# VectorE's compound tasks split in the plan, one set of eight PSUM banks, and a new order for every engine

## The chip, the cores and the metric

The kernel runs on one core of a Trainium2 chip. A core has engines with an instruction stream each: TensorE (PE in the profile, its weight loads PEld), VectorE (DVE), ScalarE (ACT), GpSimd (POOL) and SyncE (SP), which issues the DMAs. [...] The metric is the device time of one execution in microseconds, the median of several runs.

## The reference

Four attention layers in the order A, B, A, B on a sequence of S = 2048 rows of D = 512, each as `x = x + layer(layernorm(x))`, with H = 32 heads of Dh = 16. A and B have weights of their own, used twice.

```python
# A: each row looks at 8 rows, 2 apart, back from itself (W, dil = 8, 2)
idx = pos[:, None] - (jnp.arange(W) * dil)[None, :]
logits = jnp.where(idx >= 0, einsum("bhsd,bhswd->bhsw", q, kg) * Dh**-0.5, -1e9)
o = einsum("bhsw,bhswd->bhsd", softmax(logits), vg)
# B: each row looks at the last 256 rows
mask = (i - j >= 0) & (i - j < 256)
p = softmax(where(mask, einsum("bhqd,bhkd->bhqk", q, k) * Dh**-0.5, -1e9))
o = einsum("bhqk,bhkd->bhqd", p, v)
# both: o reshaped to [S, D] @ wo
```

## The kernel before

The sequence is cut into chunks of C = 256 rows. For layers 0 and 1, and then for layers 2 and 3, the program runs over the 8 chunks: A of a chunk, then B of it, so there are 16 pairs of stages A0, B0 to A7, B7 and on (after a preparation of the weights in pA, pB and W). Products that need more than 16-bit precision are split into a high and a low half (names ending in h and l).

Both layers begin with `norm`: per 128 rows BN_STATS, BN_AGGR and a small TENSOR_SCALAR on VectorE (L811, L812, L813), a power on POOL (L816), one more small operation on VectorE (L819), then the normalised rows on ACT (L832), their transposes on TensorE (`pt`, L836) and the two halves (L841 on ACT, L842 on VectorE). `proj_t` and `proj_n` are the projections (`pq`, `pv`, `po`; L861 to L863 and L881 to L884).

Layer A multiplies q by eight shifted windows of k on VectorE or POOL (`pr`, L994), sums over a head's 16 elements on TensorE (`L`, L1002), takes a softmax over 8 (L1025 to L1039), spreads the weights on TensorE (`pb`, L1061), multiplies by v on VectorE (`pw`, L1074) and sums on POOL or VectorE (L1079 to L1083).

Layer B computes the scores twice. `sq` has a query on each partition and the keys along the row; it serves only to find each row's maximum. A task of it (L1169 and L1172, "scores") fills a tile of two PSUM banks, one per head. Of the three blocks of 128 keys that a block of queries can touch, one is wholly inside the window and the two outer ones are complementary triangles: COPY_PREDICATED (L1188) copies the needed half of the third into the first, and TENSOR_REDUCE (L1190) takes the maximum over the two remaining ones (`m`). In a layer's first chunk a fused operation (L1183) does both. The maxima are transposed (L1200), split (L1205 or L1207, L1210) and go by way of DRAM into extra rows of the stacked operands `stk`. `sk` (L1257 and L1259) computes the same scores with a key on each partition and the maximum already subtracted, again into two banks; ACT takes the exponential (`p`, L1263), POOL clears what is outside the window (L1272), and TensorE multiplies by v (`av`, L1289), where a column of ones yields the sum of the weights. The result leaves PSUM by ACT (`os`, L1324) and is divided on its way through DRAM (L1349, L1363), rounded into two halves (L904, L906), and goes into the output projection.

The order is not that of the code. Each piece is put into `Plan` as a task with an engine, an assumed duration in us, the values that it reads and writes, and the buffers that it touches. The table `ORDER` gives each task its place on its engine, by stage; a negative number puts it on the task's other engine (`alt`). `order()` then plays the engines through with the assumed durations and emits the tasks one by one, so that each engine's order is the table's, and the buffers are handed out in the planned order of time. `LAG` is the time until another engine sees an end, `TURN` and `TO_ROWS` what a change of the kind of matmul costs (kinds "F", "R", "C", "H": full projections, row-tiled scores, column-tiled sums, half). `IDLE` = 110 tasks of three unused matmuls (L1398) fill TensorE near the start and the end.

PSUM has eight banks. Before the change they are two pools: `q_sc`, two tiles of two banks, for `sq` and `sk`, and `q_pj`, four tiles of one bank, for everything else:

```python
for name, bufs in (("q_sc", 2), ("q_pj", 4)):
    pool(name, bufs, bass.MemoryType.PSUM)
```

A task of VectorE could hold several instructions that follow each other: L1188 and L1190 were one, of 1.06 us; so were L811 to L813; L1025 and L1026; and L1029 to L1031.

Of the kernel before, what the change touches and what calls it, by code (L numbers as in the profile page):

```python
# [424 lines left out]
LAG = {"PE": 0.23, "DVE": 0.13, "ACT": 0.16, "POOL": 0.1, "SP": 0.0}  # L425
RATE = 0.33
SLOW = 0.25
TURN, TO_ROWS = 0.09, 0.165
RECENT, WARM, EDGE = 3.4, 0.31, 0.05


# [1006 lines left out]
```

## Time and profile before

| | |
|---|---|
| median of 3 runs | 1503.04 us (1502.67 to 1504.06) |
| span of the profiled execution, first to last instruction | 1498.1 us |
| the execution's own time beside the span | not listed; the median stands 4.9 us above the span |
| mean granted TensorE clock | 0.964 of full speed |
| TensorE / VectorE / ACT / POOL busy | 1385.4 / 1248.6 / 735.9 / 672.2 us |
| HBM | 57 GB/s over the span |

An engine's row gives busy time, its share of the span and the number of instructions. A group's row gives line, engine, operation, output<-inputs, shapes and count, then busy us and mean ns of one, then idle us ahead of it and what ended that idle time. In an answer on waits, "PE sk L1257 <- DVE m L1190" means that TensorE stood idle ahead of L1257 until VectorE's L1190 had ended. "issue" is idle time for which no release is seen. In a timeline a row has start, duration, engine and operation; "x2" merges two in a row. [...]

### The profile page before, as it was taken

The numbers are of one execution on the slowest core, as the hardware profiler recorded it, in microseconds if no ns is written. First come the engines' busy times: TensorE is split into PE (matmuls) and PEld (weight loads), VectorE is DVE, ScalarE is ACT, GpSimd is POOL, SyncE is SP. The second block draws the span as 40 slices with busy tenths as digits, with TensorE's granted clock in tenths as the row PEclk, the third lists the DMA queues.
The fourth block names the chain that finished last, engine by engine and source line by source line (L and its number), as shares of the span: only waits on it lengthen the run. The fifth ranks groups of instructions, "written<-read, shape, count | busy, mean of one in ns | idle before, by whom it ended". The sixth has DMA issues, their size and how long they took to land. (4 is left out here: it accounts for less than half of the span.)

```text
span 1498.1 us, 35059 instructions
## 1 busy us (share of the span) xinstructions
PE 1385.4 (92%) x14058; PEld 779.0 (52%) x14058; DVE 1248.6 (83%) x2332; ACT 735.9 (49%) x1052; POOL 672.2 (45%) x764
## 2 busy tenths in 40 slices
PE   6899999989899999989999898989989899999988
PEld 4574636546364554636456363745536365463534
DVE  7869797988979889897988879797887979889674
ACT  5432435545455554554555434555544554554554
POOL 2505263552816435282553617274363725527232
PEclk9799979999999999999999998999989999999999
DMA  6130212222221221222122131212212221222311
GB/s 211 43 101 21 73 34 70 61 57 70 50 93 39 75 59 51 69 58 83 42 67 69 49 93 41 88 37 74 65 40 76 63 80 41 66 63 48 93 42 44
DMA packets 89218, 97.38 MB, mean 65 GB/s; under 512 B 34016, under 2 KB 60128, under 8 KB 89056
## 3 DMA queue, kind: packets, MB, share of 16 engines
q1 hardware_dynamic: 88800, 94.89, 22.4%
q8 instruction: 110, 1.80, 0.5%
q14 instruction: 52, 0.43, 0.1%
q10 hardware_dynamic: 256, 0.26, 0.1%
HBM read 50.33 MB, written 35.09 MB: 57 GB/s over the span
## 5 line engine op out<-in xcount | busy, mean ns | idle before, releaser
L1263 ACT ACTIVATE p<-sk,sclB 128x768 f32<-128x768 f32 x480 | 425.2, 899 | 321.4 <-PE sk L1259 293.2
L1272 POOL TENSOR_SCALAR_AFFINE_SELECT p<-p 128x1024 f32<-128x1024 f32 x240 | 263.7, 1104 | 550.0 <-ACT p L1263 512.2
L1190 DVE TENSOR_REDUCE m<-sq 128x2 f32<-128x512 f32 x448 | 310.3, 693 | 15.4
L1188 DVE COPY_PREDICATED sq<-maskt,sq 128x256 f32<-128x256 int16 x448 | 189.1, 422 | 94.8 <-PE sq L1172 89.2
L1289 PE MATMUL av<-p,v 128*32 128x128 f32 (+1 forms) x3840 | 198.1, 332 | 3.4 <-POOL p L1272 1.5
L994 DVE TENSOR_TENSOR pr<-kv,q 128x512 f32<-128x512 f32 x230 | 165.4, 776 | 40.1 <-ACT kv L975 31.3
L1257 PE MATMUL sk<-stk,stk 64*128 64x256 f16 x960 | 135.8, 285 | 38.9 <-DVE m L1190 23.1
L1289 PEld LDWEIGHTS av<-p,v 128*32 128x32 f32 x3840 | 105.4, 110 | 95.4 <-issue 41.4
L1074 DVE TENSOR_TENSOR pw<-pb,kv 128x1024 f32<-128x1024 f32 x128 | 152.1, 1211 | 2.2 <-PE pb L1061 1.3
L1169 PE MATMUL sq<-stk,stk 48*128 48x128 f16 (+1 forms) x896 | 113.5, 254 | 30.5 <-DVE m L1190 18.9
L1081 POOL TENSOR_TENSOR pw<-pw 128x512 f32<-128x512 f32 x101 | 128.2, 1269 | 16.9 <-DVE pw L1074 16.7
L1257 PEld LDWEIGHTS <-stk 64*128 64x128 f16 x960 | 53.2, 94 | 157.6 <-issue 96.4
L1172 PE MATMUL sq<-stk,stk 48*128 48x128 f16 (+1 forms) x1024 | 127.5, 251 | 6.7 <-DVE m L1183 5.7
L1169 PEld LDWEIGHTS <-stk 48*128 48x128 f16 x896 | 49.2, 94 | 125.8 <-issue 83.9
L1259 PE MATMUL sk<-stk,stk 64*128 64x128 f16 x960 | 108.0, 222 | 0.0
L832 ACT ACTIVATE xn<-x,rs 128x512 f32<-128x512 f32 x64 | 52.0, 813 | 76.4 <-DVE rs L819 67.2
L1082 POOL TENSOR_TENSOR pw<-pw 128x256 f32<-128x256 f32 x101 | 74.8, 740 | 7.9
L1324 ACT COPY os<-av 128x512 f32<-128x512 f32 x60 | 34.9, 582 | 83.3 <-PE av L1289 83.1
L1002 PE MATMUL L<-pr,sel 128*32 128x512 f32 x512 | 71.6, 602 | 0.3 <-DVE pr L994 0.2
L861 PE MATMUL pq<-xh,wA0h 128*128 128x256 f16 x256 | 70.8, 276 | 0.0
L861 PE MATMUL pq<-xh,wA2h 128*128 128x256 f16 x256 | 70.7, 276 | 0.1
L862 PE MATMUL pq<-xl,wA0h 128*128 128x256 f16 x256 | 70.3, 275 | 0.3 <-DVE xl L842 0.3
(187 smaller groups left out, 3123.2 us busy)
## 6 DMA issues: line engine op xcount, KB each, us to landing
stk<-re SPq DMA_DIRECT2D x256, 96.0 KB
re<-eh SPq DMA_DIRECT2D x128, 128.0 KB
re<-el SPq DMA_DIRECT2D x64, 128.0 KB
oc<-os SPq DMA_DIRECT2D x120, 64.0 KB
os<-scr SPq DMA_DIRECT2D x15, 512.0 KB
x<-in_A_x_dram SPq DMA_DIRECT2D x8, 512.0 KB
xd<-x SPq DMA_DIRECT2D x16, 256.0 KB
x<-xd SPq DMA_DIRECT2D x8, 512.0 KB
```

The source lines that it names most:

```text
L861: nc.tensor.matmul(ps[mp].t[:, i], wh, xh, start=k == 0, stop=False)
L994: E.tensor_mul(pr.t, window(kv[1].t, m, 64 * tq, 64)[:, 0], qb)
L1074: nc.vector.tensor_mul(pw.t, pb.t.unsqueeze(1).broadcast_to([P, 2, W, 64]), v)
L1081: E.tensor_add(t[:, :, 0:4], t[:, :, 0:4], t[:, :, 4:8])
L1169: nc.tensor.matmul(ps.t[:, par, 0 : (2 - qb) * P], lhs, stk[hf, bef][r, col, qb * P :], start=True, stop=True)
L1172: nc.tensor.matmul(ps.t[:, par, (2 - qb) * P : 3 * P], lhs, stk[hf, now][r, col, : (1 + qb) * P], start=True, stop=True)
L1188: nc.vector.copy_predicated(t[:, :, 0:P], maskt[:, 0:P].bitcast(I16).unsqueeze(1).broadcast_to([P, 2, P]), t[:, :, 2 * P : 3 * P])
L1190: nc.vector.tensor_reduce(out=m.t[:, :, u, qb], in_=t[:, :, 0 : 2 * P], op=ALU.max, axis=AX.X)
L1257: nc.tensor.matmul(o[:, two], k[:, jf * P : (jf + 1) * P], q, start=True, stop=True)
L1263: nc.scalar.activation(pt.t[:, :, 2 * i : 2 * i + 2].rearrange("p s m q -> p m s q"), ps.t[:, :, : 3 * P].rearrange("p m (s q) -> p m s q" ...
L1272: nc.gpsimd.affine_select(out=v, in_=v, pattern=[[0, 8], [-1 if b == 0 else 1, P]], compare_op=ALU.is_gt if b == 0 else ALU.is_ge, fill=0. ...
L1289: nc.tensor.matmul(o, v[:, jj, 17 * h : 17 * h + 32], rhs, start=z == 0 and (b == 0 or first), stop=z == 1 and b == 1, tile_position=(0, 3 ...
```

## The change

VectorE's compound tasks become one task per instruction, so that the order can put other instructions between them: L1188 (`pick`) and L1190 (`top`); BN_STATS and BN_AGGR, with L813 now one instruction for both halves instead of two; and the five instructions of layer A's softmax. The plan's own constants change with it: `AGAIN` is the extra time of a task that follows its own engine's result, and `LEAVE` replaces `TURN` and `TO_ROWS` by a cost for each kind of matmul that is left. The two PSUM pools become one tile of eight banks. A `Banks` buffer asks for one bank or two neighbouring ones, and `order()` chooses them with `find` when the task begins in the plan: the banks that come free first, and among equals a single one that has taken neighbours. All numbers of `ORDER` are new. What is computed stays the same, and `IDLE` stays 110.

```diff
 ORDER = {
-    "pA": [1, 0, 2, -4, 0, 1, 5, 4, 7, 6, 11, 5, 10, 3, -5, 4, 2, 3, 5, 9, 9, 13, 42, 10, 15, 11, 16, 6, 8, 5, -7, 10,
...
-TURN, TO_ROWS = 0.09, 0.165
+LEAVE = {"C": 0.185, "H": 0.19, "R": 0.13, "F": 0.105, "": 0.0}
+AGAIN = {"PE": 0.0, "DVE": 0.11, "ACT": 0.12, "POOL": 0.055, "SP": 0.0}
...
+class Banks(Buf):
+    def __init__(self, psum, wide, shape):
+        self.key, self.cap, self.group, self.need = "banks", 0, 0, 0
+        self.left, self.held, self.until, self.wide, self.at = 0, False, 0.0, wide, None
+        def make():
+            if wide == 2:
+                return psum[:, self.at : self.at + 2]
+            v = psum[:, self.at]
+            return v if len(shape) == 2 else v.rearrange("p (a b) -> p a b", a=shape[1])
...
+def find(banks, wide, at):
+    best, score, where = math.inf, 0, None
+    for b in range(9 - wide):
+        free = max(banks[b : b + wide])
+        if free == math.inf:
+            continue
+        t, k = max(at, free), b
+        if wide == 1:
+            side = (b > 0 and banks[b - 1] < math.inf) + (b < 7 and banks[b + 1] < math.inf)
+            k = 100 * side + 7 - b
+        if t < best - 1e-6 or t < best + 1e-6 and k < score:
+            best, score, where = t, k, b
+    return best, where
...
-                x.ready = max(x.ready, t.end if x.eng == t.eng and not t.size else landed)
+                x.ready = max(x.ready, t.end + AGAIN[t.eng] if x.eng == t.eng and not t.size else landed)
...
-                us += 0.0 if t.mode == mode else TO_ROWS if t.mode == "R" else TURN
+                us += 0.0 if t.mode == mode else LEAVE[mode]
...
-    for name, bufs in (("q_sc", 2), ("q_pj", 4)):
-        pool(name, bufs, bass.MemoryType.PSUM)
+    psum = ctx.enter_context(tc.tile_pool(name="psum", bufs=1, space=bass.MemoryType.PSUM)).tile([P, 8, 512], F32, name="banks")
...
-            plan.add("DVE", 1.0, lambda t=t: stats(t), r=[vx[t]], w=[vmv[t], vr0[t], Val(b6)])
-        plan.add("POOL", 0.72, rstd, r=vr0[:2], w=[vr0[2]])
+            plan.add("DVE", 0.61, lambda t=t: stats(t), r=[vx[t]], w=[vb6[t]])
+            plan.add("DVE", 0.11, lambda t=t: aggr(t), r=[vb6[t]], w=[vmv[t]])
+        plan.add("DVE", 0.075, spread_, r=vmv, w=[vr0[0]])
+        plan.add("POOL", 0.72, rstd, r=[vr0[0]], w=[vr0[1]])
...
-                    ps = buf("q_sc", [P, 2, 512], F32, "sc", f"sq{l}_{c}_{j}_{u}_{qb}")
+                    ps = Banks(psum, 2, [P, 2, 512])
...
+                    def pick(ps=ps):
+                        t = ps.t
+                        nc.vector.copy_predicated(t[:, :, 0:P], maskt[:, 0:P].bitcast(I16).unsqueeze(1).broadcast_to([P, 2, P]),
+                                                  t[:, :, 2 * P : 3 * P])
+
+                    if not first:
+                        vpk = Val(ps)
+                        plan.add("DVE", 0.34, pick, r=[vps], w=[vpk])
+                        vps = vpk
+                    plan.add("DVE", 0.28 + 2 * (3 * P - x0) / 960 if first else 0.61, top, r=[vps], w=[v])
```

VectorE, in stage B5 of the first pair of layers, at the maxima of its last quarter of the heads (`m_5_3`; `b_7`, `mv_7` and `xl_7` are the norm of chunk 7, `el_6` is a projection of chunk 6). Before:

```order
L811 BN_STATS b_7_8018<-x_7_7955 128x6
L812 BN_AGGR mv_7_8020<-b_7_8018 128x2
L813 TENSOR_SCALAR rs_7_8022<-mv_7_8020 128x1
L1105 SCALAR_TENSOR_TENSOR el_6_1_8064<-pq_6_1_1_7908,eh_6_1_8013 128x2x256
L1105 SCALAR_TENSOR_TENSOR el_6_1_8064<-pq_6_1_0_7916,eh_6_1_8013 128x2x256
L819 SCALAR_TENSOR_TENSOR rs_7_8022<-mv_7_8020,rs_7_8022 128x2
L1210 SCALAR_TENSOR_TENSOR mt_5_2_8051<-mr_5_2_8044,mt_5_2_8051 128x32
L1188 COPY_PREDICATED sq_5_3_3_0_8030<-maskt,sq_5_3_3_0_8030 128x2x128
L1190 TENSOR_REDUCE m_5_3_8091<-sq_5_3_3_0_8030 128x2
L1188 COPY_PREDICATED sq_5_3_0_1_8080<-maskt,sq_5_3_0_1_8080 128x2x128
L1190 TENSOR_REDUCE m_5_3_8091<-sq_5_3_0_1_8080 128x2
L842 TENSOR_TENSOR xl_7_8133<-pt_7_0_8105,xh_7_8116 128x4x128
```

The same place now; L1284 is the COPY_PREDICATED, L1280 the TENSOR_REDUCE, L888, L891 and L894 the norm's three:

```order
L891 BN_AGGR mv_7_7396<-b_7_7378 128x2
L888 BN_STATS b_7_7378<-x_7_7317 128x6
L891 BN_AGGR mv_7_7396<-b_7_7378 128x2
L894 TENSOR_SCALAR rs_7_7412<-mv_7_7396 128x2
L1198 SCALAR_TENSOR_TENSOR el_6_1_7367<-banks,eh_6_1_7353 128x2x256
L1280 TENSOR_REDUCE m_5_3_7421<-banks 128x2
L900 SCALAR_TENSOR_TENSOR rs_7_7412<-mv_7_7396,rs_7_7412 128x2
L1284 COPY_PREDICATED banks<-maskt,banks 128x2x128 x2
L1280 TENSOR_REDUCE m_5_3_7421<-banks 128x2 x2
L925 TENSOR_TENSOR xl_7_7468<-banks,xh_7_7456 128x4x128 x2
L1284 COPY_PREDICATED banks<-maskt,banks 128x2x128
L1280 TENSOR_REDUCE m_5_3_7421<-banks 128x2
```

Two copies now stand ahead of their two maxima, and a projection's remainder stands between a maximum and the copy that belongs to it; some pairs still follow each other directly.

TensorE in the same stage, where scores are put between the projections of chunk 6 (`xh_6`, weights `wB0` and `wB1`). Each row of a score stands for one of two row halves; the second of each is left out. Before:

```order
L863 MATMUL pq_6_0_0_8076<-xh_6_7877,wB0l 128x256
L1169 LDWEIGHTS stk_0_122
L1169 MATMUL sq_5_3_0_1_8080<-stk_1_123,stk_0_122 128x128
...
L1172 MATMUL sq_5_3_0_1_8080<-stk_2_124,stk_0_122 128x256
...
L861 LDWEIGHTS wB0h
L861 MATMUL pq_6_0_0_8076<-xh_6_7877,wB0h 128x256
```

Now (L1262 and L1265 are `sq`, L1356 and L1358 `sk`, L944 to L946 the projection):

```order
L946 MATMUL banks<-xh_6_7217,wB1l 128x256
L1262 LDWEIGHTS stk_0_120
L1262 MATMUL banks<-stk_1_121,stk_0_120 128x128
...
L1265 MATMUL banks<-stk_2_122,stk_0_120 128x256
...
L1356 LDWEIGHTS stk_2_119
L1356 MATMUL banks<-stk_0_117,stk_2_119 128x2x128
...
L1358 MATMUL banks<-stk_0_117,stk_2_119 128x128
...
L944 LDWEIGHTS wB1h
L944 MATMUL banks<-xh_6_7217,wB1h 128x256
```

A single score task stood between two projections; now an `sq` and an `sk` task stand together. Their tiles are two-bank parts of `banks`.

More of the change, by code (lines that the diff above doesn't have):

```diff
@@ L446, in t @@
         return self.tile
+class Banks(Buf):
[7 more added lines that the diff above has]
+            return v if len(shape) == 2 else v.rearrange("p (a b) -> p a b", a=shape[1])
+        self.make, self.tile = make, None
+def find(banks, wide, at):
[11 more added lines that the diff above has]
+    return best, where
 class Val:
@@ L504, in order @@
                 slots.setdefault(b.key, [0.0] * b.cap)
+                taken.setdefault(b.key, 0)
                 if b.need is None:
@@ L508, in order @@
         taken = dict.fromkeys(taken, 0)
+        banks = [0.0] * 8
         for q in queue.values():
@@ L520, in begins @@
                 return math.inf
-            at, need = max(until[e], t.ready), {}
+            at, need, left = max(until[e], t.ready), {}, None
             for b in t.bufs:
                 if not b.held:
+                    if b.key == "banks":
+                        left = left or banks[:]
+                        at, z = find(left, b.wide, at)
+                        if z is None:
+                            return math.inf
+                        left[z : z + b.wide] = [math.inf] * b.wide
+                        continue
                     if taken[b.key] < b.need:
@@ L538, in leave @@
                 b.until = max(b.until, landed)
-                if not b.left:
+                if not b.left and b.key == "banks":
+                    banks[b.at : b.at + b.wide] = [b.until] * b.wide
+                elif not b.left:
                     slots[b.key].append(b.until)
@@ L558, in order @@
                     b.held = True
+                    if b.key == "banks":
+                        b.at = find(banks, b.wide, now)[1]
+                        banks[b.at : b.at + b.wide] = [math.inf] * b.wide
+                        continue
                     taken[b.key] += 1
@@ L811, in stats, with aggr, spread_ @@
             nc.vector.bn_stats(b6.t[:, t], xb.t[:, t])
+        def aggr(t):
             nc.vector.bn_aggr(mv.t[:, t], b6.t[:, t])
-            nc.vector.tensor_scalar(rs.t[:, 0, t : t + 1], mv.t[:, t, 1:2], 1.0e-5, 1.0 / (XS * XS), op0=ALU.add, op1=ALU.mult)
+        def spread_():
+            nc.vector.tensor_scalar(rs.t[:, 0], mv.t[:, :, 1], 1.0e-5, 1.0 / (XS * XS), op0=ALU.add, op1=ALU.mult)
         def rstd():
@@ L821, in norm @@
         for t in range(2):
-            plan.add("DVE", 1.0, lambda t=t: stats(t), r=[vx[t]], w=[vmv[t], vr0[t], Val(b6)])
-        plan.add("POOL", 0.72, rstd, r=vr0[:2], w=[vr0[2]])
-        plan.add("DVE", 0.08, shift, r=[vr0[2], *vmv], w=[vrs])
+            plan.add("DVE", 0.61, lambda t=t: stats(t), r=[vx[t]], w=[vb6[t]])
+            plan.add("DVE", 0.11, lambda t=t: aggr(t), r=[vb6[t]], w=[vmv[t]])
+        plan.add("DVE", 0.075, spread_, r=vmv, w=[vr0[0]])
+        plan.add("POOL", 0.72, rstd, r=[vr0[0]], w=[vr0[1]])
+        plan.add("DVE", 0.08, shift, r=[vr0[1], *vmv], w=[vrs])
         for t in range(2):
-            pts = buf("q_pj", [P, 4, P], F32, "pj", f"pt{l}_{c}_{t}")
+            pts = Banks(psum, 1, [P, 4, P])
             xn = buf("pxn", [P, D], F32, "xn", f"xn{l}_{c}_{t}")
@@ L848, in proj_t @@
         d = st8[l, c]
-        ps = [buf("q_pj", [P, 2, C], F32, "pj", f"pq{l}_{c}_{s}_{mp}") for mp in range(2)]
+        ps = [Banks(psum, 1, [P, 2, C]) for mp in range(2)]
         vps = [Val(x) for x in ps]
@@ L1025, in top, with less @@
             nc.vector.tensor_reduce(out=mx.t[:, 0], in_=src_.t.rearrange("p w t -> p t w"), op=ALU.max, axis=AX.X)
+        def less():
             nc.vector.tensor_sub(e.t, src_.t, mx.t[:, 0:1].broadcast_to([P, W, 64]))
@@ L1029, in bottom, with over, scaled @@
             nc.vector.tensor_reduce(out=mx.t[:, 1], in_=e.t.rearrange("p w t -> p t w"), op=ALU.add, axis=AX.X)
+        def over():
             nc.vector.reciprocal(mx.t[:, 0], mx.t[:, 1])
+        def scaled():
             nc.vector.tensor_mul(e.t, e.t, mx.t[:, 0:1].broadcast_to([P, W, 64]))
@@ L1043, in half @@
             return v.rearrange("p (w t) -> p w t", w=W)
-        plan.add("DVE", 1.33, top, r=[vsrc], w=[vt0, vmx])
+        vrx, vov = Val(mx), Val(mx)
+        plan.add("DVE", 0.615, top, r=[vsrc], w=[vmx])
+        plan.add("DVE", 0.61, less, r=[vsrc, vmx], w=[vt0], mode="S" if c == 0 else "")
         plan.add("ACT", 0.63, lambda: nc.scalar.activation(e.t, e.t, AF.Exp, scale=scl["A", 1]), r=[vt0, vscl["A", 1]], w=[vt1])
-        plan.add("DVE", 2.33, bottom, r=[vt1, vmx], w=[ve])
+        plan.add("DVE", 0.98, bottom, r=[vt1], w=[vrx])
+        plan.add("DVE", 0.47, over, r=[vrx, vmx], w=[vov])
+        plan.add("DVE", 0.61, scaled, r=[vt1, vov], w=[ve], mode="S")
         plan.add("ACT", 0.48, lambda: nc.scalar.copy(eh.t, e.t), r=[ve], w=[veh])
@@ L1130, in layer_b @@
         for t in range(2):
-            pv = buf("q_pj", [P, D], F32, "pj", f"pv{l}_{c}_{t}")
+            pv = Banks(psum, 1, [P, D])
             vps = Val(pv)
@@ L1186, in top @@
                         else:
-                            t = ps.t
-                            nc.vector.copy_predicated(t[:, :, 0:P], maskt[:, 0:P].bitcast(I16).unsqueeze(1).broadcast_to([P, 2, P]),
-                                                      t[:, :, 2 * P : 3 * P])
-                            nc.vector.tensor_reduce(out=m.t[:, :, u, qb], in_=t[:, :, 0 : 2 * P], op=ALU.max, axis=AX.X)
-                    plan.add("DVE", 0.28 + 2 * (3 * P - x0) / 960 if first else 1.06, top, r=[vps], w=[v])
+                            nc.vector.tensor_reduce(out=m.t[:, :, u, qb], in_=ps.t[:, :, 0 : 2 * P], op=ALU.max, axis=AX.X)
+                    def pick(ps=ps):
[7 more added lines that the diff above has]
+                    plan.add("DVE", 0.28 + 2 * (3 * P - x0) / 960 if first else 0.61, top, r=[vps], w=[v])
             mr = buf("psm", [P, 32], F32, "mr", f"mr{l}_{c}_{j}")
@@ L1393 @@
     for i in range(IDLE):
-        junk = buf("q_pj", [P, 2 * P], F32, "pj", f"idle{i}")
+        junk = Banks(psum, 1, [P, 512])
         def idle(junk=junk):
             for _ in range(3):
-                nc.tensor.matmul(junk.t, selt[:, 0], selt.rearrange("p g k -> p (g k)"), start=True, stop=True)
+                nc.tensor.matmul(junk.t[:, 0 : 2 * P], selt[:, 0], selt.rearrange("p g k -> p (g k)"), start=True, stop=True)
         plan.add("PE", 0.33, idle, w=[Val(junk)], mode="F", act=0.32)
```

15 lines of the change are left out of this document (8 added, 7 removed), and 793 rows, old and new, of the table ORDER.

## The prediction

> **What bounds the kernel now.** I read the page's first part, then the stages, then TensorE's waits, then single instructions in one stretch of the middle. The page's busy line and the stages (columns as the header says; "PEld" is the weight load):
>
> ```profile
> PE 1385.4 (92%) x14058; PEld 779.0 (52%) x14058; DVE 1248.6 (83%) x2332; ACT 735.9 (49%) x1052; POOL 672.2 (45%) x764
> core 0: us, PE busy (x) PEld busy (x) DVE busy (x) ACT busy (x) POOL busy (x), PEclk, DMA share, GB/s
> 0.00:100.00 100.00, 81.31 (x553) 54.66 (x554) 75.54 (x152) 49.13 (x73) 30.28 (x58) 0.91 0.36 115
> 100.00:1400.00 1300.00, 1222.01 (x12529) 682.74 (x12527) 1112.29 (x2066) 637.65 (x916) 611.63 (x679) 0.97 0.22 61
> 1400.00:1498.10 98.10, 82.07 (x981) 41.56 (x979) 60.79 (x115) 49.09 (x63) 30.27 (x28) 0.98 0.22 61
> ```
>
> In the 1300 us of the middle TensorE is busy for 94% and VectorE for 86%; ACT and POOL are at half. No engine is full: TensorE is the bound, with 78 us in which it stands still (1300 - 1222), and VectorE is close behind. So a shorter VectorE pays only where TensorE waits for it. TensorE's waits, longest first (us in total, times, longest):
>
> ```profile
> PE sk L1257 <- DVE m L1190: 23.1, 39, 1.9
> PE sq L1169 <- DVE m L1190: 18.9, 33, 1.9
> PE sk L1257 <- ACT p L1263: 12.4, 25, 1.0
> PE sq L1169 <- ACT p L1263: 9.8, 22, 1.1
> ...
> PE sq L1172 <- DVE m L1183: 5.7, 10, 1.6
> ...
> PE sk L1257 <- DVE m L1183: 1.6, 4, 0.9
> ...
> PE sq L1172 <- ACT p L1263: 0.8, 2, 0.5
> ```
>
> All seven are the same thing: a score task (sq or sk) wants a two-bank PSUM tile that its last reader, VectorE's maximum or ACT's exponential, has not left. They sum to 72.3 us in 135 waits: 49.3 us in 86 waits for VectorE (0.57 us each), 23.0 us in 49 for ACT (0.47 us each). That is what the change can win by waits.
>
> The second thing is inside TensorE's busy time. These rows are the place of the TensorE order shown above:
>
> ```profile
> 604.74 0.27 PE L862 MATMUL pq<-xl,wB0h 128*128 128x256 f16 x1
> 604.85 0.27 PE L863 MATMUL pq<-xh,wB0l 128*128 128x256 f16 x1
> 605.05 0.10 PEld L1169 LDWEIGHTS <-stk 48*128 48x128 f16 x2 [0.21 <-issue]
> 605.05 0.23 PE L1169 MATMUL sq<-stk,stk 48*128 48x128 f16 x2
> 605.12 0.27 PE L1172 MATMUL sq<-stk,stk 48*128 48x256 f16 x2
> 605.32 0.10 PEld L861 LDWEIGHTS <-wB0h 128*128 128x128 f16 x1 [0.16 <-issue]
> 605.32 0.28 PE L861 MATMUL pq<-xh,wB0h 128*128 128x256 f16 x1
> ```
>
> A 256-column matmul follows its like after 0.11 us (604.74 to 604.85). From a projection to a score it is 0.20 us, and back (605.12 to 605.32) also 0.20 us: a turn between kinds of matmul costs 0.09 us each way, with nothing waited for but "issue".
>
> **The change, part by part.**
>
> *VectorE's single instructions.* The same place on VectorE:
>
> ```profile
> 602.81 0.65 DVE L811 BATCH_NORM_STATS2 b<-x 128x6 f32<-128x512 f32 x1
> 603.50 0.18 DVE L812 BATCH_NORM_AGGREGATE mv<-b 128x2 f32<-128x6 f32 x1
> 603.72 0.15 DVE L813 TENSOR_SCALAR rs<-mv 128x1 f32<-128x1 f32 x1
> 603.79 1.28 DVE L1105 SCALAR_TENSOR_TENSOR el<-pq,eh 128x512 f16<-128x512 f32 x2
> ...
> 605.15 0.42 DVE L1188 COPY_PREDICATED sq<-maskt,sq 128x256 f32<-128x256 int16 x1
> 605.61 0.69 DVE L1190 TENSOR_REDUCE m<-sq 128x2 f32<-128x512 f32 x1
> 606.22 0.42 DVE L1188 COPY_PREDICATED sq<-maskt,sq 128x256 f32<-128x256 int16 x1
> ```
>
> L1190 reads what L1188 writes, and starts 0.04 us after its end (605.57, 605.61). The next L1188 reads nothing of L1190, and starts 0.08 us before its end (606.30, 606.22). The difference is 0.12 us between records rounded to 0.01; the next pair, 606.22+0.42 and 606.67, would give 0.11, and I take 0.11 us per instruction that stands directly behind the one it waits for. Counted in the two programs, 871 VectorE instructions wait for the one directly ahead of them before, 472 after: 399 x 0.11 = -44 us of VectorE. Of that, 270 of the 448 pairs of L1188 and L1190 are parted, which is 30 us; the rest lies mostly in the norm's chain.
>
> *Work that changes engine.* Counted by line in the orders, VectorE gets 6 more L1207, 3 more L1039, 8 more L906 and one more L1363, and loses 2 of L994 and some weight preparation:
>
> ```profile
> L994 DVE TENSOR_TENSOR pr<-kv,q 128x512 f32<-128x512 f32 x230 | 165.4, 776 | 40.1 <-ACT kv L975 31.3 <-PE L L1002 7.9 <-ACT q L973 0.5
> L1363 DVE TENSOR_TENSOR oc<-oc,os 128x512 f32<-128x512 f32 x19 | 16.6, 889 | 2.2 <-DMA os<-scr 2.2
> L906 DVE TENSOR_TENSOR ol<-oc,oh 128x512 f16<-128x512 f32 x7 | 6.4, 923 | 3.7 <-ACT oh L904 3.6
> L1207 DVE TENSOR_SCALAR mt<-mr 128x32 f16<-128x32 f32 x15 | 5.1, 338 | 0.3
> L1039 DVE TENSOR_TENSOR e<-e,eh 128x512 f16<-128x512 f32 x7 | 4.8, 691 | 0.0
> L733 DVE CUSTOM_DVE_ANT_0 wA0l<-stk 128x1024 bf16<-128x1024 f32 x1 | 1.2, 1220 | 0.0
> L786 DVE TENSOR_SCALAR wA2h<-stk,pscA 128x1024 f16<-128x1024 f32 x1 | 0.8, 752 | 0.0
> ```
>
> 6 x 0.338 + 3 x 0.691 + 8 x 0.923 + 0.889 = +12.4; 2 x 0.776 + 1.22 + 2 x 0.752 = -4.3; and 32 fewer L813, at 0.07 each (603.72 to 603.79), -2.2: together +6 us. VectorE's net is -38 us of 1249. POOL and ACT, half idle, hide their side; without that cover it is under 12 us.
>
> *Turns on TensorE.* Changes of kind between neighbouring matmuls in TensorE's order: 1439 before, 1313 after, 126 fewer, of which 112 are between projections and scores. At 0.09 us that is -11 us; the remaining kinds of turn have no row here, and at twice the price for all of them it would be -23 us. TensorE has these turns in its busy time, so they lie on the path almost whole; I take -12.
>
> *One set of eight banks.* Before, a score tile is reused after two score tasks; in TensorE's orders a score's banks are taken again after 25.0 matmuls on average before, 29.9 after (counted with the bank numbers of the plan). 4.9 x 0.11 = 0.54 us more for the reader to leave. Against it, parting the pairs holds banks longer: 461 instructions stand between the two halves of the 270 parted pairs, at about 0.45 us (between 0.34, an L1188 less its overlap, and 0.61, an L1190 to its follower) some 207 us over 448 tiles, 0.46 us each. So for sq tiles the longer reuse and the longer hold nearly cancel, and only the 38 us that VectorE is shorter remain; for sk tiles, read by ACT, the 0.54 us exceed the mean wait of 0.47 us. I take two thirds of ACT's 23.0 (-15) and a fifth of VectorE's 49.3 (-9): -24 us. The bounds are -72 (all seven rows gone) and a loss, below. What is late next is ACT's and POOL's part of the sk chain.
>
> *Waits in the instruction streams.* The bank set brings 179 more wait instructions on ACT, 87 more on VectorE and 43 fewer on TensorE (counted in the programs); nearly all name a reader that TensorE's own wait has already covered. Their price:
>
> ```profile
> L1263 ACTq EVENT_SEMAPHORE  x173: 17/17/38, 140.0 to 1478.6; - x173
> L1188 DVEq EVENT_SEMAPHORE  x295: 21/21/4341, 182.9 to 1465.9; - x148
> ```
>
> 179 x 17 ns + 87 x 21 ns is under 5 us, mostly while the engine waits anyway: 0. Start, filler matmuls (110 tasks in both) and the last output's chain have the same instructions: 0, with 5 us to either side for their new order.
>
> **The sum.** 1498.1 - 12 - 24 = 1462 us of span; the runs' median of 1503.0 is 4.9 us above that span, which stays: 1467 us, 2.4% faster.
>
> **The rivals.**
>
> *VectorE's gain does not reach TensorE.* Scores then wait as long as before, at other places; for it speaks that VectorE has about 190 us of idle in the middle already (1300 - 1112) and TensorE waits all the same. Only the turns remain: 1503 - 12 = 1491.
>
> *Nothing is gained by putting an instruction between.* If an instruction always began after the last had emptied, parting pairs would save nothing, VectorE would stand at 1249 + 4, and an order laid for gaps that do not exist would keep the old waits: 1503 - 12 = 1491 again. Against it stands the 0.08 us by which L1188 starts ahead of L1190's end. [...]
>
> *Slower: banks held through parted pairs.* A tile stays taken while VectorE does other work between L1188 and L1190; 90 of the parted pairs have two or more instructions between. If 15% of the 207 us of holding ends as a TensorE wait, that is +31, and the 72 us of waits do not fall: 1503 - 12 + 31 = 1522. It decides from 12 of 207 us (6%) on if the other waits stay, from 36 (17%) if they fall as I forecast. For it: 9% of the 992 score tasks wait for VectorE now (86), and accumulators and projections now take banks out of the same set, in which a score needs two neighbours. Against it: the reuse distance grew in the order in spite of that.
>
> *It cancels.* Holding gives back just what the turns win: 1503.
>
> **How the numbers follow.** Forecast 0.58; gain not reaching TensorE 0.10; no gain from parting 0.04; slower 0.24; cancels 0.04. About 0.2%, 3 us, is what a measurement of this kernel tells from no change. Faster 0.58 + 0.10 + 0.04 = 0.72, same 0.04, slower 0.24. For the range: at the low end two thirds of the 72 us (48) and 23 for the turns give 1432, and I leave 0.07 below it; at the high end 1515 leaves about half of the slower case, 0.13, above. Within the forecast alone the range is 1440 to 1488.
>
> **What the changed profile would show.** VectorE: the maximum's two instructions apart, the first followed by a stranger after about 0.34 us instead of 0.46, busy time plus idle lower. TensorE: fewer waits of 0.16 to 0.21 us put down to issue, and the seven rows at about 48 us in sum instead of 72. Middle: TensorE at 95 to 96% busy. Wrong it would be if the waits of scores for the maximum grow above 60 us, if the wait moves to TensorE's weighted sums behind POOL's masks, or if the granted clock in the middle falls below 0.95.

## The result

The changed kernel takes 1461.5 us (median of 4, 1460.2 to 1463.9) against 1502.9 us: a ratio of 0.9724 (95% interval 0.9710 to 0.9738), 41.4 us less. The forecast was 1467 us, within a range of 1432 to 1515.

The page's busy line of the changed kernel, whose span is 1458.5 us:

```profile
PE 1365.3 (94%) x14058; PEld 792.0 (54%) x14058; DVE 1210.2 (83%) x2312; ACT 738.7 (51%) x1050; POOL 660.9 (45%) x754
```

Its stages, columns as the header says:

```profile
core 0: us, PE busy (x) PEld busy (x) DVE busy (x) ACT busy (x) POOL busy (x), PEclk, DMA share, GB/s
0.00:100.00 100.00, 79.57 (x562) 54.66 (x563) 75.79 (x153) 52.47 (x78) 30.05 (x59) 0.95 0.39 119
100.00:1360.00 1260.00, 1196.44 (x12383) 685.80 (x12383) 1068.11 (x2032) 632.38 (x901) 596.94 (x664) 0.97 0.23 63
1360.00:1458.50 98.50, 89.28 (x1121) 51.57 (x1117) 66.30 (x130) 53.86 (x71) 33.93 (x31) 1.00 0.24 68
```

VectorE has 1210.2 us of work instead of 1248.6, 38.4 less. TensorE does the same 14058 matmuls in 1365.3 us instead of 1385.4 and stands still for 1458.5 - 1365.3 = 93.2 us instead of 112.7. In the middle it is 95% busy (1196.44 of 1260), where it was 94%. So the 39.6 us of span are 20.1 of busy time and 19.5 of idle time.

TensorE's waits of the changed kernel, longest first (us in total, times, longest):

```profile
PE banks L1356 <- DVE m L1280: 11.4, 27, 1.5
PE banks L1497 <- POOL selt L750: 7.5, 1, 7.5
PE banks L1356 <- DVE pw L1167: 6.7, 8, 1.7
PE banks L1262 <- DVE m L1280: 6.6, 17, 1.2
PE banks L1356 <- ACT p L1362: 6.0, 14, 1.0
PE banks L1388 <- POOL p L1371: 5.7, 12, 1.8
PE banks L919 <- ACT xn L915: 5.6, 5, 2.8
PE banks L1262 <- ACT p L1362: 4.9, 14, 0.8
...
PE banks L1262 <- DVE pw L1167: 2.0, 5, 0.8
PE banks L1265 <- DVE m L1276: 1.6, 7, 0.3
```

The scores (L1262, L1265 and L1356) wait for VectorE's maxima 20 us in all (11.4 + 6.6 + 1.6, and 0.5 in a smaller row) instead of 49.3, and for ACT's exponentials 10.9 instead of 23.0: 31 us where the forecast had 48. The weighted sums (L1388) wait 5.7 us for POOL's masks, where it was 1.5; that sign of being wrong shows, but small. Something new stands beside them: scores now wait for readers that used to have banks of their own, above all VectorE's products of layer A (`pw`, 6.7 + 2.0). All idle time ahead of the score lines went from 76.1 to 49.6 us. The groups that show it, from the page:

```profile
L1280 DVE TENSOR_REDUCE m<-banks 128x2 f32<-128x512 f32 x448 | 300.4, 686 | 6.1
L1284 DVE COPY_PREDICATED banks<-maskt,banks 128x256 f32<-128x256 int16 x448 | 181.4, 422 | 84.9 <-PE banks L1265 80.2
L1356 PE MATMUL banks<-stk,stk 64*128 64x256 f16 x960 | 138.2, 282 | 28.7 <-DVE m L1280 11.4
L1265 PE MATMUL banks<-stk,stk 48*128 48x128 f16 (+1 forms) x1024 | 127.4, 249 | 4.0 <-DVE m L1276 1.6
L1262 PE MATMUL banks<-stk,stk 48*128 48x128 f16 (+1 forms) x896 | 112.5, 252 | 16.9 <-DVE m L1280 6.6
```

The copy takes as long as before (422 ns) and the maximum nearly so (686 ns after 693); what is gone is the time between them. VectorE at two places of the stage shown in the section on the change (start us, us):

```profile
595.90 0.41 DVE L1284 COPY_PREDICATED banks<-maskt,banks 128x256 f32<-128x256 int16 x1
596.22 0.18 DVE L891 BATCH_NORM_AGGREGATE mv<-b 128x2 f32<-128x6 f32 x1
...
603.60 0.42 DVE L1284 COPY_PREDICATED banks<-maskt,banks 128x256 f32<-128x256 int16 x1
604.06 0.69 DVE L1280 TENSOR_REDUCE m<-banks 128x2 f32<-128x512 f32 x1
```

Behind a copy, an instruction that doesn't need it starts after 0.32 us (595.90 to 596.22); the copy's own maximum starts after 0.46 us (603.60 to 604.06). And TensorE in the same stage:

```profile
602.40 0.27 PE L946 MATMUL banks<-xh,wB0l 128*128 128x256 f16 x1
602.60 0.28 PE L1356 MATMUL banks<-stk,stk 64*128 64x256 f16 x2
602.72 0.22 PE L1358 MATMUL banks<-stk,stk 64*128 64x128 f16 x2
602.78 0.27 PE L1262 MATMUL banks<-stk,stk 48*128 48x256 f16 x2
602.89 0.22 PE L1265 MATMUL banks<-stk,stk 48*128 48x128 f16 x2
603.04 0.28 PE L944 MATMUL banks<-xh,wB0h 128*128 128x256 f16 x1
```

The gap of 0.20 us from a projection to a score (602.40 to 602.60) is now paid for two score tasks at once; between these a start follows the last by 0.06 us (602.72 to 602.78).

### The profile page after: what moved, and what is told of

It is laid out like the page before. It is cut to its first block, busy times and chain, and to the rows that moved or that the text cites. A ratio compares the mean times of both kernels' runs of the same rounds, so it can differ in the third digit from the quotient of the medians.

```text
span 1458.5 us, 35237 instructions
## 1 busy us (share of the span) xinstructions
PE 1365.3 (94%) x14058; PEld 792.0 (54%) x14058; DVE 1210.2 (83%) x2312; ACT 738.7 (51%) x1050; POOL 660.9 (45%) x754
## 4 chain that ended last, share of the span: by engine, by line
PE 56%; DVE 23%; POOL 8%; issue 6%; DMA 3%; ACT 3%; SPq 1%; ACTq 0%; DVEq 0%; POOLq 0%
PE banks L944 9%; PE banks L945 8%; PE banks L946 8%; PE banks L1388 6%; DVE m L1280 5%; PE banks L1085 4%; PE banks L1356 4%; PE banks L966 3%; DVE pw L1167 3%; PE banks L964 3%; DVE banks L1284 3%; PE banks L967 3%; POOL pw L1174 3%; PE banks L1262 3%; PE banks L919 2%
## 5 line engine op out<-in xcount | busy, mean ns | idle before, releaser
L1362 ACT ACTIVATE p<-banks,sclB 128x768 f32<-128x768 f32 x480 | 420.8, 900 | 263.4 <-PE banks L1358 198.0
L1280 DVE TENSOR_REDUCE m<-banks 128x2 f32<-128x512 f32 x448 | 300.4, 686 | 6.1
L1284 DVE COPY_PREDICATED banks<-maskt,banks 128x256 f32<-128x256 int16 x448 | 181.4, 422 | 84.9 <-PE banks L1265 80.2
L1388 PE MATMUL banks<-p,v 128*32 128x128 f32 (+1 forms) x3840 | 196.0, 331 | 7.0 <-POOL p L1371 5.7
L1356 PE MATMUL banks<-stk,stk 64*128 64x256 f16 x960 | 138.2, 282 | 28.7 <-DVE m L1280 11.4
L1388 PEld LDWEIGHTS banks<-p,v 128*32 128x32 f32 x3840 | 106.2, 109 | 99.7 <-issue 36.2
L1167 DVE TENSOR_TENSOR pw<-banks,kv 128x1024 f32<-128x1024 f32 x128 | 153.3, 1212 | 2.8 <-PE banks L1154 1.2
L1265 PE MATMUL banks<-stk,stk 48*128 48x128 f16 (+1 forms) x1024 | 127.4, 249 | 4.0 <-DVE m L1276 1.6
L1262 PE MATMUL banks<-stk,stk 48*128 48x128 f16 (+1 forms) x896 | 112.5, 252 | 16.9 <-DVE m L1280 6.6
L1356 PEld LDWEIGHTS <-stk 64*128 64x128 f16 x960 | 56.5, 94 | 114.3 <-issue 108.5
L1358 PE MATMUL banks<-stk,stk 64*128 64x128 f16 x960 | 109.7, 221 | 0.0
L1262 PEld LDWEIGHTS <-stk 48*128 48x128 f16 x896 | 50.7, 94 | 104.9 <-issue 98.1
L944 PE MATMUL banks<-xh,wB1h 128*128 128x256 f16 x256 | 70.7, 276 | 0.1
L944 PE MATMUL banks<-xh,wA2h 128*128 128x256 f16 x256 | 70.6, 276 | 0.0
L944 PE MATMUL banks<-xh,wA0h 128*128 128x256 f16 x256 | 70.6, 276 | 0.0
L946 PE MATMUL banks<-xh,wA0l 128*128 128x256 f16 x256 | 70.2, 274 | 0.2 <-DVE wA0l L864 0.2
```

The source lines that it names most:

```text
L944: nc.tensor.matmul(ps[mp].t[:, i], wh, xh, start=k == 0, stop=False)
L946: nc.tensor.matmul(ps[mp].t[:, i], wl, xh, start=False, stop=k == 3)
L1167: nc.vector.tensor_mul(pw.t, pb.t.unsqueeze(1).broadcast_to([P, 2, W, 64]), v)
L1262: nc.tensor.matmul(ps.t[:, par, 0 : (2 - qb) * P], lhs, stk[hf, bef][r, col, qb * P :], start=True, stop=True)
L1280: nc.vector.tensor_reduce(out=m.t[:, :, u, qb], in_=ps.t[:, :, 0 : 2 * P], op=ALU.max, axis=AX.X)
L1284: nc.vector.copy_predicated(t[:, :, 0:P], maskt[:, 0:P].bitcast(I16).unsqueeze(1).broadcast_to([P, 2, P]), t[:, :, 2 * P : 3 * P])
```

## The experiments

The theory was the forecast's: the shorter VectorE and the shared banks shorten the scores' waits, and fewer turns shorten TensorE's busy time. The rivals: it is only the new order; parting the pairs holds banks and costs; the turns have no price. Each ratio is to the kernel before, run beside it on the same chip. The time given first is the run's own median; a difference is taken from the ratio times 1502.9, so it need not be the difference of the medians, and "+41" is against the changed kernel's 1461.5 where this is said. A difference between two runs that were each set against the kernel before is known to about 3 to 5 us.

**The pairs put together again.** In the changed kernel each copy is moved down to directly ahead of its maximum.

```diff
+        line = queue["DVE"][::-1]
+        for t in [x for x in line if x.fn.__name__ == "pick"]:
+            top = next(x for x in t.after if x.fn.__name__ == "top")
+            line.remove(t)
+            line.insert(line.index(top), t)
+        queue["DVE"] = line[::-1]
```

> The changed kernel with every copy moved directly ahead of its maximum on VectorE again (270 parted pairs rejoined); the orders of the other engines, the bank set and everything else as changed. VectorE becomes about 270 x 0.11 = 30 us longer, and two-bank tiles are held for less time. Forecast's theory (a shorter VectorE reaches the end only by a share of TensorE's waits, about a quarter): +7 us, 1468. Rival 1, VectorE's gain does not reach TensorE: 1461 within 3. Rival 2, VectorE sets the pace: +30, 1491.

Measured: 1502.5, ratio 0.9998 (0.9987 to 1.0008): +41 against the changed kernel, all of the gain, and more than any of the three expectations (0, +7, +30). Its TensorE waits (the code stands six lines lower, so L1362 is the `sk` line, L1268 the `sq` line and L1286 the maximum), then its span and mean granted clock:

```profile
PE banks L1362 <- DVE m L1286: 27.9, 44, 3.2
PE banks L1268 <- DVE m L1286: 14.3, 28, 1.6
```

```profile
core 0: 1505.1 us, clock 0.955
```

The waits for the maxima doubled, from 18.0 (11.4 + 6.6) to 42.2 us. But that the parting is worth 41 us doesn't follow: copies now also start later than their places in the order. The next run was made to see how much of it is VectorE's time alone.

**VectorE's time without a moved instruction.** In the changed kernel the maximum runs over 288 columns instead of 256, which takes in 32 keys more.

```diff
-  in_=ps.t[:, :, 0 : 2 * P], op=ALU.max, axis=AX.X)
+  in_=ps.t[:, :, 0 : 2 * P + 32], op=ALU.max, axis=AX.X)
```

> The changed kernel with its own order, pairs parted, and each maximum taken over 288 instead of 256 columns per head (32 more keys, which may lie outside the window; the softmax is scaled by another maximum). VectorE is 448 x 64/960 = 30 us longer, as when the pairs were rejoined, with no instruction moved. Theory 1, the 41 us that rejoining cost are VectorE's time: +30 to +41, 1491 to 1502. Theory 2, VectorE's time reaches the end by 0.42 as with the shorter copy in the kernel before (19 of 45 us): +13, 1474; then the rest of the 41 is that rejoining moves copies behind other work.

Measured: 1476.0, ratio 0.9829 (0.9803 to 0.9856): +15.8 against the changed kernel at an unchanged order of VectorE's instructions. The maximum's group went from 300.4 to 330.4 us (64 columns more, 0.067 us for each of the 448), so a microsecond in that group costs 0.53. VectorE's whole busy time, in which records that overlap count once, rose by 26.1 (1210.2 to 1236.3); by that it is 0.61. The waits:

```profile
PE banks L1356 <- DVE m L1280: 16.8, 39, 1.5
...
PE banks L1262 <- DVE m L1280: 9.4, 22, 1.4
```

By this price, the 30 us of the 270 rejoined pairs are 16 of the 41 us. The other 25 or so come with the copies' later places.

**The same from the other side.** In the kernel before, the copy covers 80 instead of 128 columns and leaves part of the window out of the maxima.

```diff
-  nc.vector.copy_predicated(t[:, :, 0:P], maskt[:, 0:P].bitcast(I16).unsqueeze(1).broadcast_to([P, 2, P]),
-                            t[:, :, 2 * P : 3 * P])
+  nc.vector.copy_predicated(t[:, :, 0:80], maskt[:, 0:80].bitcast(I16).unsqueeze(1).broadcast_to([P, 2, 80]),
+                            t[:, :, 2 * P : 2 * P + 80])
```

> The kernel before, its order untouched, with the copy ahead of the maximum cut from 128 to 80 columns (so the maxima leave out part of the window; the softmax is scaled by another maximum). VectorE is shorter by 448 x 0.1 = 45 us and nothing else changes. Forecast's theory: about a quarter reaches the end, -11, 1492. Rival 1, nothing reaches TensorE: 1503 within 3. Rival 2, VectorE sets the pace: -45, 1458.

Measured: 1482.8, ratio 0.9876 (0.9860 to 0.9892), -18.6. The copy's group, before and in this run:

```profile
L1188 DVE COPY_PREDICATED sq<-maskt,sq 128x256 f32<-128x256 int16 x448 | 189.1, 422 | 94.8 <-PE sq L1172 89.2 <-ACT p L1263 2.8 <-ACT kv L975 0.6
L1188 DVE COPY_PREDICATED sq<-maskt,sq 128x160 f32<-128x160 int16 x448 | 144.5, 322 | 103.2 <-PE sq L1172 97.1 <-ACT p L1263 2.8 <-ACT xn L832 0.9
```

44.6 us of this group are worth 18.6: 0.42 each, with the old order, the old pools and no pair parted. VectorE's whole busy time fell by 39.3 (1248.6 to 1209.3); by that it is 0.47, about twice the forecast's quarter. So about half of VectorE's time reaches the end. The rest VectorE spends idle, 8.4 us of it in longer waits for scores ahead of the copies (94.8 to 103.2).

**The same cut in the changed kernel**, which leaves the same part out:

```diff
-  t[:, :, 2 * P : 3 * P])
+  t[:, :, 2 * P : 2 * P + 80])
```

> The changed kernel with the copy cut from 128 to 80 columns (the maxima leave out part of the window), so that VectorE is 45 us shorter once more. By the slopes so far (0.42 in the kernel before, 0.48 upward in the changed one): -20, 1441. If TensorE, now 95% busy in the middle, leaves less to win: -10 or less, 1451 or more.

Measured: 1450.5, ratio 0.9672 (0.9641 to 0.9704): -11 against the changed kernel's own median, -7.8 by the two ratios (0.9672 against 0.9724). 43.9 us less in the copy's group are worth 0.18 each now by the ratios, 0.06 to 0.3 with their intervals; by VectorE's whole busy time (38.0 less) it is 0.21. Its page:

```profile
PE 1358.6 (94%) x14058; PEld 788.5 (54%) x14058; DVE 1172.2 (81%) x2312; ACT 737.9 (51%) x1050; POOL 661.4 (46%) x754
```

VectorE falls to 81% while TensorE stays at 94%: a microsecond of VectorE brings less than half of what it brought before.

**Turns alone.** In the kernel before, 208 parts of projections are exchanged with a score task beside them, so that each stands between two score tasks: 1855 turns instead of 1439.

```diff
+TURNED = [220, 229, 332, 344, 369, 384, 397,
...
+        line = queue["PE"]
+        for i in TURNED:
+            i = len(line) - 1 - i
+            line[i], line[i - 1] = line[i - 1], line[i]
```

> The kernel before, with 208 times one projection part moved between two neighbouring score tasks on TensorE: 1855 changes of kind instead of 1439, the second score 0.33 us later each time. Forecast's theory (0.09 us a turn, almost wholly on the path): 416 x 0.09 = +37, 1540. Rival, turns hide in TensorE's idle time: under +10. Above +60 the later scores would cost more than the turns.

Measured: 1531.0, ratio 1.0194 (1.0177 to 1.0210), +29.2 for 416 turns: 0.070 us each. Its page, and its clock:

```profile
PE 1425.0 (93%) x14058; PEld 758.4 (50%) x14058; DVE 1249.2 (82%) x2332; ACT 735.0 (48%) x1052; POOL 672.5 (44%) x764
```

```profile
core 0: 1530.2 us, clock 0.964
```

TensorE's busy time rose by 39.6 us (1425.0 - 1385.4) at the clock of before, 0.095 us per turn, as the timeline's 0.09 said. Its idle time fell by 7.5 (112.7 to 105.2); I put that down to a slower TensorE waiting less.

**The bank set alone.** The kernel before, with its own order and its compound tasks, but with the eight banks as one set.

```diff
-    for name, bufs in (("q_sc", 2), ("q_pj", 4)):
-        pool(name, bufs, bass.MemoryType.PSUM)
+    psum = ctx.enter_context(tc.tile_pool(name="psum", bufs=1, space=bass.MemoryType.PSUM)).tile([P, 8, 512], F32, name="banks")
...
-                    ps = buf("q_sc", [P, 2, 512], F32, "sc", f"sq{l}_{c}_{j}_{u}_{qb}")
+                    ps = Banks(psum, 2, [P, 2, 512])
```

> The kernel before with its own order and its compound tasks, only the two PSUM pools replaced by the one set of eight banks. Forecast's theory (a score tile is reused later, the waits for ACT's exponential shrink by two thirds): -15 us, 1488. Rival 1, the set pays only with an order made for it: 1503 within 3. Rival 2, accumulators and projections take banks that scores need: 1510 or more.

Measured: 1499.9, ratio 0.9976 (0.9962 to 0.9990), -3.6. Its TensorE waits (L1214 and L1302 are the score lines, L1235 and L1228 the maxima, L1308 the exponential, L1334 the weighted sum, L1317 POOL's mask):

```profile
PE banks L1302 <- DVE m L1235: 17.5, 29, 2.2
PE banks L1214 <- DVE m L1235: 13.3, 24, 2.1
PE banks L1334 <- POOL p L1317: 10.2, 12, 2.5
...
PE banks L1214 <- ACT p L1308: 7.1, 15, 1.0
...
PE banks L1302 <- ACT p L1308: 5.9, 11, 1.0
...
PE banks L1217 <- DVE m L1228: 4.0, 9, 1.9
```

The scores' waits fell as forecast: for ACT from 23.0 to 13.0, for the maxima from 49.3 to 34.8. They came back elsewhere, such as 10.2 us of the weighted sums behind POOL's masks (1.5 before): TensorE's idle time is 119.4 us in all (1497.8 - 1378.4), 6.7 more than before. The set in the old order removes waits of the scores and hardly any of TensorE.

**Holding a tile.** In the changed kernel the maximum is moved up to directly behind its copy, so that a tile is freed as early as it can be.

```diff
+            top = next(x for x in t.after if x.fn.__name__ == "top")
+            line.remove(top)
+            line.insert(line.index(t) + 1, top)
```

> The changed kernel with the 270 parted pairs rejoined the other way: the maximum moved up directly behind its copy. VectorE is 30 us longer as in the first rejoining, but each two-bank tile comes free earlier, and the work that stood between comes later. Theory 1 (VectorE's time): 1491 to 1502. Theory 2 (moved copies): nearer 1474. Rival, longer holds hurt in the changed kernel: under 1474.

Measured: 1520.2, ratio 1.0117 (1.0093 to 1.0141): +59 against the changed kernel, more than with the copies moved down and more than any expectation had. TensorE's waits (L925 is a transpose of the norm's rows):

```profile
PE banks L1362 <- DVE m L1286: 24.7, 34, 2.8
PE banks L925 <- ACT xn L921: 21.4, 21, 2.8
PE banks L1268 <- DVE m L1286: 12.3, 20, 1.9
```

Freeing the tiles sooner didn't help. What the maxima pushed back is late instead: the transposes wait 21.4 us for normalised rows, whose statistics come from VectorE, instead of 5.6.

**Pairs parted in the old order**, first with the old pools (129 exchanges of a maximum with the instruction behind it, 176 pairs parted), then with the bank set (138 exchanges, 195 pairs).

```diff
+PART = {2, 8, 11, 13, 17, 19, 24, 29, 33,
...
+        for t in [x for x in reversed(line) if x.fn.__name__ == "pick"]:
+            n += 1
+            i = line.index(t)
+            if n in PART:
+                line[i - 1], line[i - 2] = line[i - 2], line[i - 1]
```

> The kernel before, own order and pools, with copy and maximum as two tasks and 129 times the maximum and the instruction behind it exchanged, where that was ready: 176 of 448 pairs are parted. VectorE is 176 x 0.11 = 19 us shorter. By the slope of the shorter copy (19 of 45 us): -8, 1494. If parting holds tiles too long with two score tiles: 1503 or more. If VectorE's time counts in full: -19, 1483.

> The kernel before's order with the bank set and 195 of 448 pairs parted in the same way. VectorE is 195 x 0.11 = 21 us shorter. If the two parts add: -2 from the set and -9 from parting, 1491. If the bank set is what lets parting pay: 1482 or less. If both are worth only what the order makes of them: 1500 or more.

Measured: 1515.7, ratio 1.0089 (1.0067 to 1.0111), with the pools; 1501.2, ratio 0.9996 (0.9980 to 1.0011), with the set. By 0.42 a microsecond, 176 x 0.11 = 19 us of VectorE should have brought -8; the time rose by 13. So either a parted pair costs because it holds its banks longer, or the exchange itself costs. The next two runs were made for that.

**Exchanges that rejoin nothing and change no work.** In the changed kernel, and then in the kernel before, 129 pairs of independent neighbours of VectorE's order change places.

```diff
+SWAPPED = [20, 50, 60, 66, 72, 78, 82, 91,
...
+        line = queue["DVE"]
+        for i in SWAPPED:
+            i = len(line) - 1 - i
+            line[i], line[i - 1] = line[i - 1], line[i]
```

> The changed kernel with 129 pairs of independent neighbours on VectorE exchanged, chosen at random among those that were ready; no pair of copy and maximum is rejoined, and as many instructions as before (330 of the plan's tasks) stand directly behind one they wait for, so VectorE has the same work. Theory, the order itself carries the rest of the gain (rejoining cost 27 us beyond VectorE's time for 270 moved copies, parting in the old order about 21 us for 129 exchanges): 0.10 to 0.16 us each, +13 to +21, 1474 to 1482. Rival, only the copies' places and the holding of tiles matter: 1461 within 3.

> The kernel before, tasks and pools untouched, with 129 pairs of independent neighbouring tasks on VectorE exchanged at random among those that were ready; VectorE has the same work. In the changed kernel the same disturbance cost 30 us. If the old order was fitted as closely as the new one: +20 to +40, 1523 to 1543, and the new order's fit is no gain over the old one's. If the old order was looser, so that closeness of fit is part of the gain: +10 or less, 1513 or less.

Measured: 1488.9, ratio 0.9922 (0.9895 to 0.9950), +30 against the changed kernel; and 1521.0, ratio 1.0134 (1.0104 to 1.0164), +20 against the kernel before. VectorE's busy time is that of the kernels they came from (1211.2 and 1249.5). TensorE's waits of the first:

```profile
PE banks L1361 <- DVE m L1285: 18.5, 28, 3.1
PE banks L924 <- ACT xn L920: 10.8, 12, 3.3
PE banks L1361 <- DVE pw L1172: 9.7, 9, 4.2
```

An exchange costs 0.23 us in the new order and 0.16 in the old, with no work added. 129 exchanges at 0.16 (+20) and -8 for VectorE come to +12, where the pools with parted pairs measured +13: by this price nothing is left over for holding. With the bank set the same sum doesn't come out (22 - 9 = +13 against the set alone, measured +3 by the two ratios), so the price of an exchange isn't a constant, and the first agreement may be chance. The two sets of exchanges were drawn at random, so +30 against +20 doesn't show whether the new order is the more closely fitted.

**The rest of the pairs parted** in the changed kernel: 37 more exchanges, 139 pairs together instead of 178.

```diff
+PART = {385, 263, 264, 140, 141, 144, 284,
...
+            if n in PART:
+                line[i - 1], line[i - 2] = line[i - 2], line[i - 1]
```

> The changed kernel with 37 more exchanges behind a copy and its maximum, which leaves 139 pairs together instead of 178: VectorE is about 34 x 0.11 = 4 us shorter. VectorE's time alone: -2, 1460. With what exchanges cost an order (0.10 to 0.16 us each): +2 to +4, 1463 to 1465.

Measured: 1476.9, ratio 0.9839 (0.9816 to 0.9861): +17 against the changed kernel, 0.5 us per exchange, though VectorE has some 4 us less to do. Why these cost twice what the others do isn't settled. No kernel that computes everything ran faster than the changed one.

## Why the prediction was right, and where not

Two sums of the gain can be made. The first is that of the two profiled executions. I take busy time multiplied by the granted clock for what TensorE had to do at full speed:

| kernel | busy us | clock | product | idle us |
|---|---|---|---|---|
| before | 1385.4 | 0.964 | 1335.5 | 112.7 |
| before, exchanges | 1396.9 | 0.956 | 1335.4 | 121.7 |
| before, short copy | 1378.1 | 0.969 | 1335.4 | 105.9 |
| before, bank set | 1378.4 | 0.972 | 1339.8 | 119.4 |
| before, more turns | 1425.0 | 0.964 | 1373.7 | 105.2 |
| after | 1365.3 | 0.971 | 1325.7 | 93.2 |
| after, exchanges | 1372.7 | 0.966 | 1326.0 | 112.6 |
| after, pairs together | 1389.4 | 0.955 | 1326.9 | 115.7 |

With one order and one layout of the banks the product hardly moves (1335.4 to 1335.5 in three rows of the kernel before, 1325.7 to 1326.9 in the three of the changed one), but with the turns it does (1373.7). The row of the bank set stands 4.3 above that of before with the same matmuls in the same order, so the product is good to some 4 us. From before to after it falls by 9.8, which is 10 us of time; the clock's step from 0.964 to 0.971 is another 10 of the busy time, and idle time gives 19.5: together the 39.6 us of span. The clock's part is that of these two executions. The kernel before had clocks from 0.959 to 0.972, 0.965 in the mean of the 46 executions beside the experiments, and the changed kernel 0.9685 in the mean of 4; that difference is worth about 5 us.

The second sum is by cause, from the experiments: VectorE's 38.4 us of busy time at 0.47 to 0.61 (the slopes by busy time) give -18 to -23, 126 turns at 0.070 to 0.095 give -9 to -12, the set alone -3.6. That is -31 to -39 of -41.4, with slopes that the runs' intervals leave open by 13% (0.47) and 28% (0.61). The remaining 2 to 11 us belong to the new order and the set together, or to the gaps named in the second point below, and weren't separated. With the new order and the two fixed pools `order()` finds no allotment of banks and gets stuck, so no run shows the order without the set.

- *Turns, -12.* Right: -10 by the product, -9 to -12 by the price measured.
- *VectorE's net of -38 us.* The mechanism is right: behind a copy a stranger starts after 0.32 us, as said (0.34). That busy time fell by just 38.4 (1248.6 to 1210.2) is partly luck. The 0.11 us were counted from start to start, so they hold the gap of some 0.03 us ahead of a dependent instruction, which busy time leaves out. In the two traces there are 836 such gaps of at most 0.06 us, 28.6 us in sum, and then 414 of 14.0. With them VectorE is 53 us shorter: 46 by overlaps and gaps, where the forecast had 44, and 7 by shorter instructions, where it had 6 us more. By 0.47 to 0.61, 53 us would be -25 to -32, and the second sum would leave nothing over.
- *"A fifth of VectorE's 49.3 (-9)".* Too small (and a fifth of 49.3 is 9.9). VectorE's time is worth about half of itself, -18 to -23 by the lower count, and the waits for the maxima fell by three fifths, to 20 us. I priced VectorE's gain by the rows of waits that name its maxima; but a shorter VectorE makes everything behind it earlier, not only the scores that wait for a maximum.
- *"Two thirds of ACT's 23.0 (-15)" from the longer reuse of the set.* The rows did fall (to 13.0 with the set alone, to 10.9 in the changed kernel), but as a term of the sum it was too large: the set alone gave -3.6, since other waits took their place.
- The two misses have opposite signs, so -24 for waits met -26.5 ahead of the score lines. New waits elsewhere took 7 of that back (idle time fell by 19.5), and the clock, for which the sum had no term, gave 10 in these two executions. That 1467 came within 6 us of the measured time is therefore luck in part: the parts of the change are the right ones, but of the two terms for the waits one was too small by half and the other four times too large.
- *Fewer waits of TensorE put down to issue.* Not seen. The two score lines' rows of the weight load, before and then after:

```profile
PEld L1257 <- issue: 96.4, 264, 1.2
PEld L1169 <- issue: 83.9, 245, 1.2
```

```profile
PEld L1356 <- issue: 108.5, 298, 1.9
PEld L1262 <- issue: 98.1, 300, 1.4
```

They grew, from 180.3 to 206.6 us together, while TensorE's idle time fell from 112.7 to 93.2. So time ahead of a weight load isn't TensorE's idle time here, and these rows can't count turns; TensorE's busy time times its clock can (10 us by the product).

Of the rivals, "the gain does not reach TensorE" is wrong: it does, by about half. "Nothing is gained by putting an instruction between" is wrong: the timeline shows 0.32 against 0.46 us, and VectorE is 38 us shorter. "Banks held through parted pairs" is not shown anywhere: the change is faster, tiles freed sooner made it slower (+59 against +41), and the old pools with parted pairs come out at the average price of an exchange. But every one of these runs also disturbed the order, so a small price of holding stays possible.

## What to carry to other kernels

Price an engine's saved time by its slope at the end, not by the rows of waits that name it: lengthen or shorten one frequent instruction, leave the order, divide, and measure the saved time the same way on both sides. Where a planner has fitted an order, an edit of that order by hand tests the fit before it tests the idea, so a control with as many exchanges and no change of work belongs beside it. And waits that vanish from one line are a gain only if the engine's idle time as a whole falls: with the set alone the scores waited 24.5 us less (10.0 for ACT, 14.5 for the maxima), and TensorE stood idle for 6.7 more.

## What was not expected of the hardware

With the pairs together TensorE lost time in two ways: its idle time rose by 22.5 us (115.7 - 93.2), and its busy time by 24.1 with the same matmuls in the same order; the clock's 0.955 instead of 0.971 accounts for that (1365.3 x 0.971 / 0.955 = 1388.2, measured 1389.4). Over all executions the mean clocks were 0.9585 (10) and 0.9685 (4).

The mean hides two values. In the traces of the kernel before and of the changed one every record of the clock is either 1.00 or 0.50, and half lasts 3.4 us or a small multiple of it (17.1 us at most). Two neighbouring stretches of the changed kernel, columns as in the stages:

```profile
562.40:565.80 3.40, 1.51 (x19) 0.88 (x19) 3.40 (x7) 2.29 (x3) 3.24 (x5) 1.00 0.36 57
565.80:569.20 3.40, 3.05 (x17) 0.98 (x17) 3.37 (x5) 2.56 (x4) 3.17 (x5) 0.50 0.23 48
```

TensorE is busy for 1.51 of 3.40 us, and the next stretch runs at half the clock. The changed kernel has 14 stretches of half clock up to its last matmul, 85 us, and the kernel before 15, 109 us. With the pairs together it is some 135 us, an estimate from the span and the mean clock, if half is the only other value there too (1505.1 x 0.045 x 2). In the two traces TensorE was busy for 78% or less of the 3.4 us ahead of each of these stretches, against 92 and 94% in the mean. Not every such low stretch is followed by half the clock: in the changed kernel TensorE is busy for 2.18 of 3.42 us (401.98 to 405.40), and the next 3.41 us have the full clock. So no threshold is shown, and what lowers the clock isn't either.

The sum of idle time alone doesn't decide the clock: the old order with the set and parted pairs had 118.7 us of idle time, but by the same estimate only some 93 us of half clock (1503.1 x 0.031 x 2), and the highest mean clock of all, 0.973 over ten executions.

The second surprise is how closely an order of some 2000 instructions is fitted: 129 exchanges of neighbours cost 20 to 30 us in either kernel, half or more of what the whole change won.
